# A transformer block on one Trainium2 core: fewer transposes on TensorE, other homes for the key features, and a new order

## The chip, the cores and the metric

The kernel runs on one core of one Trainium2 chip. A core has five engines that run side by side, each through its own queue in order: PE (TensorE, the matrix unit), DVE (VectorE), ACT (ScalarE), POOL (GpSimd) and SP (SyncE, which here only issues DMA transfers). PEld is the part of PE that loads weights. An instruction waits at the head of its queue until the semaphores that it names are reached, and all that stands behind it on that engine waits too. The metric is the device time of one execution, in microseconds; lower is better.

## The reference

The input x has 2048 tokens of 512 numbers. Six vectors of 512 come from silu(c) @ w_mod: sa, ca, ga for the first half and sb, cb, gb for the second.

```python
h = layernorm(x) * (1 + ca) + sa
x = x + ga * A(h)
h = layernorm(x) * (1 + cb) + sb
x = x + gb * B(h)
```

A is attention without a score matrix, with 32 heads of 16:

```python
pq, pk = q @ w_phi, k @ w_phi                      # per head
phi_q = [softmax(pq), softmax(-pq)]                # 32 features per head and token
phi_k = [softmax(pk), softmax(-pk)]
kv, z = phi_k^T v, sum over tokens of phi_k
o = (phi_q kv) / (phi_q z + 1e-6);  A = o @ wo
```

B is (sigmoid(h @ w_gate) * (h @ w_up)) @ w_down, with an inner width of 1376.

## The kernel before

The tokens are 16 tiles of 128, one token per partition. Each piece of work is a small task with a name, a list of engines that it may run on, what it reads and writes, and the buffers that it holds. The text `ORDER` lists all tasks in one sequence; a word such as `xn1_5@P` puts the task on POOL (D is DVE, A is ACT), and a word without a letter takes the first engine of the task's list. The sequence fixes the order of each engine's queue and which buffer a task gets. Nothing is decided at run time.

The stages, with the task names that the text uses (t is a token tile, j one of four blocks of 128 features, g a group of tiles):

- **Loads** `ld_*` on SP, in the order in which SP meets them; SP also issues the DMA transposes, in the same queue.
- **First normalization.** `st1_t` takes mean and variance (DVE, lines 782 and 783). `rs1_g` makes 1/std for a group of tiles, on ACT or POOL (792, 793). `nmr1_g` makes -mean/std, one small DVE instruction per tile (798). `xn1_t` normalizes a tile: on POOL as x times 1/std plus -mean/std (811), on DVE as x minus mean, times 1/std (809), on ACT with scale and bias (807).
- **Transposition and modulation.** The list `LG` says which tiles form a group and `TD` how a group is transposed: 0 by PE (`tphgj`, line 824) into PSUM, 1 by DMA (`xT1_t`, line 816) straight into h1T. Then `hm1_gj` scales and shifts block j of the whole group (831 on ACT, 833 on DVE or POOL). Groups are tiles 0, 1, and then pairs; the pairs 10/11 and 12/13 go by DMA.
- **Weights of q and k** are multiplied by w_phi first (`wTc`, `wqT`, `fold`, `foldc`).
- **Keys.** `Kt` is the key product (850), `et` two exponentials of it on ACT (866), `nt` the softmax sums on DVE (869), `rt` their reciprocals on DVE or ACT (882, 879), `phit` the multiplication of the exponentials by the reciprocals, on POOL (872). `Vt` and `vat` make the values (854, 890). `kvt` adds phi^T v into two PSUM banks (274). From tile 11 on a tile's features are made in two or four parts (`phi11.2` is the part that begins at block 2).
- **kv.** `kvm`, `kvp`, `kvz`, `kvn` mask the finished sum, permute it by a product and store it as `kvbd`.
- **Queries** `Qcb` and their exponentials `qecb` (928, 933) stand in the order wherever PE has room. `modc2` makes the second half's sb and cb, `ga` and `gb` the two gates; `wo*` and `wd*` multiply the gates into the two output weights, on POOL or DVE (908, 917).
- **Attention output.** For tiles 0 to 7 `sm`/`den` make the coefficients and `num`, `u` the weighted sums. For tiles 8 to 15 `num` also holds the denominators; `zti` copies some of its columns to SBUF (367, 369), and `dnt` makes the coefficients from them and the PSUM banks in ten DVE instructions (383 to 391). `ut..` multiplies (433, 435, 450), `ot` adds the two halves on POOL or DVE (468), `oTt` transposes (by DMA from tile 2 on), `outt` is the product with wo (477), `x1_t` the residual.
- **Second normalization and B.** `st2`, `rs2`, `nmr2` (one small DVE instruction per tile, line 504), `xn2`, `xnT`, `mod`, then per chunk of 1, 1, 2, 4, 4 and 4 tiles the products `g` and `u` (568), tanh `tg` (578), `hm` (589), the down-projection `y` (606), `fin` and the store `st`.

A second path for inputs with large scores follows behind a flag; it isn't taken here.

Of the kernel before, what the change touches and what calls it, by code (L numbers as in the profile page):

```python
# [12 lines left out]
ACT = mybir.ActivationFunctionType  # L13
ALU = mybir.AluOpType
AX = mybir.AxisListType

P = 128
# [18 lines left out]
wdz warm0 c1 warm1_0 warm1_1 warm1_2 pmem ld_x0b st1_3 st1_2 bd c2 rs1_2 warm1_3 ld_x0a st1_0 warm1_4 warm1_5 warm1_6 rs1_0 ld_wk ld_x1 st1_1 rs1_1 warm1_7  # L36
tpw3 tpw2 wTc2 tpw0 ld_wm00 ld_wm01 wTc0 tpw1 c3 wTc3@D nmr1_2 warm1_8 warm1_9 warm1_10 warm1_11 warm1_12 warm1_13 xn1_0 nmr1_1 wTc1 fold13 foldc13 xn1_2@P
fold11 fold10 tph03 tph01 fold12 foldc10 foldc11 foldc12 xn1_1@P xn1_3@P st1_5 ld_x2 st1_4 st1_6 st1_7 modc1.0 ld_wv tph02 tph23 tph21 rs1_3@P nmr1_3 modc1.1
modc1c tph20 tph13 warm1_14 tph00 hm1_20 hm1_01@A hm1_21@A hm1_03@A hm1_13 hm1_00 hm1_02 tph22 rs1_4@P nmr1_4 K0 tph10 hm1_22@A hm1_23@A K2 ld_wq st1_11 e0.0
xn1_4@P xn1_5@P xn1_6@P hm1_10@A st1_10 tph11 st1_9 st1_8 e2.0 hm1_11@A tph12 hm1_12@A V2 xn1_7@P tph31 K3 hm1_31 e3.0 tph43 tph30 K1 tph32 rs1_6@P nmr1_6  # L40
n0.0 hm1_43@A rs1_5@P nmr1_5 hm1_32 hm1_30 tph41 V0 tph33 e1.0 tph42 V1 tph40 n2.0 xn1_11@P xn1_10@P ld_x3 wqT3 ld_wo wqT0 r0.0@A hm1_33@A xn1_8@P xn1_9@P
hm1_41 va0 K5 hm1_42@A xT1_11 hm1_40@A va2 va1 tph52 K4 tph53 xT1_10 st1_13 r2.0 n1.0 phi0.0 e4.0 r1.0@A phi2.0 st1_12 tph51 tph50 V4 hm1_50@A hm1_53@A rs1_7
wqT2 phi1.0 n3.0 va4@D hm1_51 hm1_52 wqT1 nmr1_7 xn1_13@P xn1_12@P K6 n4.0 r3.0 r4.0 V3 V5 kv0.0 K7 kv1.0 kv2.0 hm1_62 hm1_61 va5 e5.0 e6.0 n5.0 va3@D e7.0
hm1_63 phi3.0 xT1_13 xT1_12 fold02 V8 r5.0 phi4.0 hm1_60 foldc02 va8 V7 V6 kv3.0 fold00 va7 st1_14 n7.0 r7.0 n6.0 K8 e8.0 phi5.0 hm1_72 K10 kv4.0 fold03 K11
warm1_15 hm1_70@P va6 r6.0@A e11.4 e11.6 hm1_71 kv5.0 phi7.0 hm1_73 n8.0 foldc00@D foldc03@D st1_15 r8.0 e11.0 phi6.0 V11 K9 e11.2 fold01 n11.6 ld_wd2 ld_wd
ld_wu perm e9.0 rs1_8 V10 K13 e13.4 n11.4 foldc01@D n11.2 n9.0 r11.6 nmr1_8 ld_wmga ld_wmm2 r9.0 kv6.0 kv7.0 phi8.0 va10 e10.0 e13.0 va11@D r11.2 V9 va9@D
r11.4 phi9.0 Q00 V12 Q03 xn1_14 xn1_15 qe00 kv8.0 Q10 phi11.2 phi11.4 kv9.0 qe03 n11.0 n10.0 tph81 tph83 phi11.6 r11.0 r10.0@A K12 hm1_81 hm1_83 tph80 tph82
Q13 hm1_82@A phi11.0 phi10.0 hm1_80 n13.0 K15 K14 r13.0 va12@D e12.0 kv10.0 e15.4 phi13.0 n13.4 r13.4@A phi13.4 e15.0 n12.0 r12.0 kv11.4 e14.0 e14.4 n15.4
n14.4 Q02 kv11.0 kv11.2 Q11 V13 ld_wg qe02 qe11 scb kv11.6 r14.4 n15.0 va13@D r15.4 n14.0 phi12.0 r14.0 r15.0 phi14.4 V14 V15 va15 va14 phi15.4 ga kv12.0
kv13.0 modc2.0 kv13.4 kv14.4 kv15.4 phi14.0 qe10 Q01 kvm1 gac kvp2 kvz2 kv14.0 phi15.0 kv15.0 qe01 Q32 kvm0 kvp1 kvp0 qe32 wo1@D wo2 kvz0 kvz1 gb kvn1@A kvn2  # L50
sm0 modc2.1 sm1 modc2c smS1 gbc kvn0 smS0@D qe13 Q12 sm2 num00 num21 num31 num01 den0 wo0 wo3 den1 Q21 qe12 smS2 wo_all wmod_free u00 u01 num11 num30 tpo0 oT0
den2 u31 u30 u11 wd4 Q31 qe31 wd0 wd2 o3 out0 num10 num20 Q23 qe21 x1_0 u10 wd7 wd1 Q30 qe23 st2_0 u21 u20 qe30 rs2_0 Q33 tpo1 sm4 smS4 nmr2_0 oT1@D xn2_0
num60 Q22 num71 qe33 den4 xnT0 out1 oT3 out3 Q20 u71 x1_1 u60 mod00@A mod02@A mod03@A mod01@A x1_3 st2_3 g0.9 g0.0 u0.9 g0.6 u0.0 o2 wd9 tsw tg0.9 tg0.0 oT2
out2 hm0.0 qe20 tg0.6 wd5 g0.5 g0.8 u0.6 wr st2_1 hm0.9 hm0.6 tg0.5 tg0.8 x1_2 u0.5 u0.7 u0.8 hm0.5 hm0.8 wd6 wd10 rs2_1 sm3 g0.1 g0.7 num61 u0.1 qe22 nmr2_1
st2_2 tg0.7 tg0.1 hm0.1 u0.4 wd3 g0.3 u0.3 tg0.3 xn2_1 g0.2 g0.10 g0.4 u61 hm0.3 hm0.7 tg0.4 tg0.2 u0.2 y0.0 rs2_2 hm0.2 nmr2_2 y0.1 xnT1 num70 o6 xn2_3@P
y0.2 y0.3 u0.10 wd8 xn2_2@P mod11 oT6 xnT3 xnT2 hm0.4 num50 y0.4 u70 smS3@D y0.5 y0.6 mod10@A tg0.10 mod13@A mod12@A u1.1 g1.1 y0.7 tg1.1 num51 g1.5 hm0.10
den3 hm1.1 g1.8 g1.9 u1.5 tg1.9 tg1.5 u51 u50 hm1.5 y0.8 y0.9 u1.8 y0.10 fin0 u1.4 g1.4 tg1.4 hm1.4 g1.0 u1.9 u1.0 num41 g1.3 num40 tg1.8 hm1.9 hm1.8 tg1.0
u1.6 u1.3 g1.2 u1.7 mod21@A tg1.3 u40 hm1.0 hm1.3 o7 mod20@A g1.6 tg1.2 tg1.6 hm1.6 u41 u1.10 g1.7 tg1.7 u1.2 o5 out6 mod22@A mod23@P g2.2 oT7 o4@D out7 x1_6
hm1.7 hm1.2 st2_6 x1_7 g2.0 g2.6 u2.0 g2.10 tg2.6 st2_7 tg2.0 st0 oT5 oT4 hm2.0 g1.10 u2.10 u2.6 tg1.10 hm2.6 hm1.10 rs2_4 nmr2_4 g2.1 u2.4 g2.4 tg2.10 hm2.10
num80 z80@D xn2_7@D tg2.4 tg2.1 hm2.4 num81 u2.1 hm2.1 num82 y1.0 out5 z81@D tg2.2 z82 dn8 x1_5 u800 y1.1 y1.2 y1.3 u2.2 hm2.2 xn2_6 xnT7 xnT6 y3.0 out4 g2.8  # L60
g2.5 u2.8 y1.4 tg2.5 y1.5 y1.6 y1.7 y1.8 y1.9 tg2.8 st2_5 x1_4 st2_4 u811 u821 hm2.8 u820 g2.7 y3.1 g2.3 u2.5 rs2_3 u2.3 mod43@A tg2.3 nmr2_3 xn2_5 xnT5 hm2.5
xn2_4@P xnT4 hm2.3 y1.10 num102 z102@D fin1 num92 tg2.7 g2.9 u2.9 num91 num90 y2.0 y2.1 y3.2 tg2.9 z91@D hm2.9 z90 z92 dn9 y3.3 y3.4 u2.7 y2.2 y3.5 y2.3 u900
u921 hm2.7 u911 mod40@P y2.4 y3.6 y2.5 num100 num101 y2.6 mod30@A z101 z100 mod31@P mod42@P mod32@P y2.7 st1 u920 num110 y2.8 y3.7 y2.9 y2.10 o9 dn10 u1021
u1000 fin2 u1011 u1020 o10 o8 y3.8 y3.9 mod33@A mod41@A g3.10 g3.8 u3.10 num130 g3.0 y3.10 tg3.10 z130 tg3.8 hm3.10 fin3 st2 oT9 u3.8 num112 hm3.8 tg3.0 z112
# [12 lines left out]
tg5.5 hm5.5 y9.8 y9.9 y9.10 u5.1 u5.0 g5.0 tg5.1 hm5.1 fin11 fin9 u5.9 u5.10 tg5.0 bndc g5.2 hm5.0 tg5.2 u5.4 g5.9 hm5.4 hm5.2 tg5.9 hm5.9 g5.10 st11 st9
tg5.10 hm5.10 bndd y13.0 y13.1 y13.2 y13.3 y12.0 y12.1 y12.2 y13.4 y13.5 y13.6 y13.7 y13.8 y13.9 y13.10 fin13 st13 y12.3 y12.4 y12.5 y12.6 y12.7 y12.8 y12.9
# [1038 lines left out]
```

## Time and profile before

| | |
|---|---|
| runs | 209.8, 211.09, 211.3 us; median 211.09 |
| the profiled execution | 209.63 us, of which 207.9 are the span from the first instruction to the last |
| PE busy | 200.3 us, 96% of the span, 1516 matmuls |
| DVE busy | 168.2 us, 81%, 459 instructions |
| ACT busy | 107.9 us, 52% |
| POOL busy | 103.4 us, 50% |
| granted PE clock | 1.00 |
| first key product, last matmul | 13.35 and 204.5 us from the start |
| last key feature tile | ends at 56.33 us |

How to read the lines that follow. A line of groups has the source line, the engine, the operation, what it writes and reads by the program's names, the shapes, how often it ran, its busy time, and the mean length of one in ns; behind the bar stands the idle time of the engine in front of it and who ended it. A line of the timeline begins with the start and the length in us. A line of waits has who waited for whom, then us in total, how often, and the longest. Two instructions that follow each other on DVE overlap by about 0.08 us in this trace, so lengths add up to a little more than the time they take.

### The profile page before, as it was taken

Reading aid. Unit: us, or ns where it says so; the run is one execution under the profiler, and the core shown is the slowest. Engines: PE = TensorE matmul, PEld = TensorE weight load, DVE = VectorE, ACT = ScalarE, POOL = GpSimd, SP = SyncE. Lnnn points to the kernel's source line nnn. Section 1 sums busy time; section 2 is a strip of 40 time slices with the busy share of each in tenths; the row PEclk is TensorE's granted clock in tenths of the full one; section 3 lists DMA queues with packets and bytes.
Section 4 is the critical chain, followed back from the end, with each engine's and each line's share of the span. In section 5 each row is a group of like instructions: output and inputs, shape, how many; then the busy total and the mean of one; then the engine's idle time right before and its main releaser. Section 6 shows DMA issues by size and latency. Waiting matters only on the chain.

```text
span 207.9 us, 4302 instructions
## 1 busy us (share of the span) xinstructions
PE 200.3 (96%) x1516; PEld 112.4 (54%) x1539; DVE 168.2 (81%) x459; ACT 107.9 (52%) x259; POOL 103.4 (50%) x137
## 2 busy tenths in 40 slices
PE   7789999999999999999999999999999999999994
PEld 2555465454675588976764544454444444444443
DVE  3999999999599998899988999979797815456642
ACT  2699999999886986524443322521244300142300
POOL 5589999999996989601337202633040612000000
PEclk9999999999999999999999999999999999999999
DMA  6995922999200201522032210342011131001011
GB/s 179 367 349 144 130 32 51 321 390 401 82 3 3 50 2 30 122 33 42 12 76 52 54 25 0 77 101 55 0 29 47 25 79 50 25 2 50 3 60 54
DMA packets 30893, 18.74 MB, mean 90 GB/s; under 512 B 20657, under 2 KB 28818, under 8 KB 30866
## 3 DMA queue, kind: packets, MB, share of 16 engines
q1 hardware_dynamic: 30336, 18.39, 31.6%
q8 instruction: 14, 0.23, 0.5%
q14 instruction: 13, 0.11, 0.2%
q10 hardware_dynamic: 530, 0.02, 0.1%
HBM read 11.58 MB, written 2.10 MB: 66 GB/s over the span
## 4 chain that ended last, share of the span: by engine, by line
PE 74%; ACT 7%; POOL 6%; DMA 4%; DVE 3%; issue 3%; SPq 1%; POOLq 0%; DVEq 0%
PE y_ps L606 18%; PE g_ps L568 17%; PE u_ps L568 17%; PE a_ps L477 6%; POOL phi L872 5%; PE q_ps L928 5%; DMA wmod_sb<-in_w_mod_dram 4%; ACT h1T L831 3%; ACT e L866 2%; DVE ks L869 2%; PE num L360 2%; PE num L444 2%; PE v_ps L854 1%; PE g_ps L570 1%; ACT tg L578 1%
## 5 line engine op out<-in xcount | busy, mean ns | idle before, releaser
L578 ACT ACTIVATE tg<-g_ps 128x512 bf16<-128x512 f32 (+4 forms) x66 | 28.7, 454 | 66.2 <-PE g_ps L568 50.5
L606 PE MATMUL y_ps<-wd_sb,wmod_sb 128*128 128x512 bf16 (+3 forms) x182 | 42.2, 366 | 0.2
L589 DVE SCALAR_TENSOR_TENSOR wmod_sb<-tg,u_ps 128x512 bf16<-128x512 bf16 (+4 forms) x63 | 30.0, 495 | 13.0 <-ACT tg L578 7.0
L872 POOL TENSOR_TENSOR phi<-e,ks 128x1024 bf16<-128x1024 bf16 (+2 forms) x22 | 31.5, 1453 | 0.5
L568 PEld LDWEIGHTS <-wu_sb 128*128 128x128 bf16 (+1 forms) x252 | 21.7, 99 | 15.4
L568 PEld LDWEIGHTS <-wg_sb 128*128 128x128 bf16 (+1 forms) x252 | 21.4, 99 | 15.2 <-issue 0.2
L606 PEld LDWEIGHTS <-wmod_sb 128*128 128x128 bf16 (+1 forms) x187 | 17.9, 98 | 16.5
L568 PE MATMUL g_ps<-wT_sb,wg_sb 128*128 128x512 bf16 (+2 forms) x121 | 23.8, 321 | 0.2
L568 PE MATMUL u_ps<-wT_sb,wu_sb 128*128 128x512 bf16 (+2 forms) x123 | 23.7, 322 | 0.1
L497 POOL TENSOR_SCALAR ve<-mv 128x2 f32<-128x2 f32 (+1 forms) x8 | 1.8, 223 | 41.2 <-DVE mv L487 41.2
L568 PE MATMUL g_ps<-wqk_sb,wg_sb 128*128 128x128 bf16 (+4 forms) x127 | 19.9, 287 | 0.1
L613 DVE TENSOR_TENSOR ot<-y_ps,x 128x512 bf16<-128x512 f32 (+1 forms) x17 | 11.1, 656 | 11.0 <-PE y_ps L606 10.5
L568 PE MATMUL u_ps<-wqk_sb,wu_sb 128*128 128x128 bf16 (+4 forms) x128 | 19.5, 287 | 0.0
L468 POOL TENSOR_TENSOR o<-u 128x512 bf16<-128x512 f32 x12 | 15.2, 1268 | 8.7 <-DVE u L435 4.7
L869 DVE TENSOR_REDUCE ks<-e 128x64 f32<-128x1024 bf16 (+2 forms) x22 | 19.4, 899 | 0.0
L866 ACT ACTIVATE e<-k_ps 128x512 bf16<-128x512 f32 (+2 forms) x44 | 18.1, 502 | 0.3 <-PE k_ps L850 0.2
L933 ACT ACTIVATE eT<-q_ps 128x512 bf16<-128x512 f32 x32 | 17.0, 622 | 1.3 <-PE q_ps L928 1.0
L850 PE MATMUL k_ps<-wqk_f,h1T 128*128 128x512 bf16 x62 | 15.8, 379 | 0.4 <-DVE h1T L833 0.3
L477 PE MATMUL a_ps<-wo_sb,oT 128*128 128x512 bf16 x61 | 15.8, 379 | 0.1
L928 PE MATMUL q_ps<-h1T,wqk_f 128*128 128x512 bf16 x58 | 15.6, 379 | 0.3
L854 PE MATMUL v_ps<-wv_sb,h1T 128*128 128x512 bf16 x62 | 15.6, 379 | 0.2
L782 DVE BATCH_NORM_STATS2 st<-x_sb 128x6 f32<-128x512 bf16 x16 | 10.7, 669 | 2.5 <-DMA x_sb<-in_A_x_dram 2.5
(158 smaller groups left out, 331.3 us busy)
## 6 DMA issues: line engine op xcount, KB each, us to landing
out_dram<-ot SPq DMA_DIRECT2D x15, 128.0 KB, 1.9
x_sb<-in_A_x_dram SPq DMA_DIRECT2D x3, 512.0 KB, 8.5
wmod_sb<-in_w_mod_dram SPq DMA_DIRECT2D x3, 512.0 KB, 7.5
wmod_sb<-in_w_mod_dram SPq DMA_DIRECT2D x1, 1536.0 KB, 14.9
wu_sb<-in_B_w_up_dram SPq DMA_DIRECT2D x1, 1376.0 KB, 9.7
wg_sb<-in_B_w_gate_dram SPq DMA_DIRECT2D x1, 1376.0 KB, 16.4
wd_sb<-in_B_w_down_dram SPq DMA_DIRECT2D x1, 1280.0 KB, 6.6
wqk_sb<-in_A_wqkv_dram SPq DMA_DIRECT2D x2, 512.0 KB, 7.6
```

The lines of the kernel that those rows point to most:

```text
L477: pe.matmul(ap_[:], lhsT=oT[:, j, :], rhs=wo_sb[:, j, :], start=(j == 0), stop=(j == KT - 1))
L568: pe.matmul(ps[:fsz, 0:n], lhsT=w[:, j, ft * P:ft * P + fsz], rhs=h[:, j, 0:n], start=(j == 0), stop=(j == KT - 1))
L578: G.add(f"tg{k}.{ft}", {"ACT": 0.13 + n * 0.00083}, lambda e, tg=tg, g_ps=g_ps, fsz=fsz, n=n: act.activation(tg[:fsz, 0:n], g_ps[:fsz, 0:n ...
L589: dve.scalar_tensor_tensor(hm_all[:fsz, hm[k].slot, ft, 0:n], tg[:fsz, 0:n], 1.0, u_ps[:fsz, 0:n], op0=ALU.add, op1=ALU.mult)
L606: mm = pe.matmul(y[:, 0:c1 - c0], lhsT=hm_all[:fsz, hm[k].slot, ft, tl * P:(tl + 1) * P], rhs=wd_sb[:fsz, ft, c0:c1], start=(ft == 0), sto ...
L850: pe.matmul(kp[:], lhsT=h1T[:, j, t * P:(t + 1) * P], rhs=wqk_f[:, j, D:2 * D], start=(j == 0), stop=(j == KT - 1))
L854: pe.matmul(vp[:], lhsT=h1T[:, j, t * P:(t + 1) * P], rhs=wv_sb[:, j, :], start=(j == 0), stop=(j == KT - 1))
L866: act.activation(ee[:, ha:hb, s, :], kp[:, ha * DH:hb * DH].rearrange("p (h j) -> p h j", j=DH), ACT.Exp, scale=1.0 - 2.0 * s)
L869: dve.tensor_reduce(ks[:, ha:hb].rearrange("p h s -> p (h s)"), ee[:, ha:hb].rearrange("p h s j -> p (h s) j"), axis=AX.X, op=ALU.add)
L872: pool.tensor_tensor(ph[:, ha * 32:hb * 32].rearrange("p (h j) -> p h j", j=DH), ee[:, ha:hb].rearrange("p h s j -> p (h s) j"), ks[:, ha: ...
L928: pe.matmul(qp[:], lhsT=wqk_f[:, j, blk * P:(blk + 1) * P], rhs=h1T[:, j, cq * 512:(cq + 1) * 512], start=(j == 0), stop=(j == KT - 1))
L933: act.activation(eT[cq][:, s * 4 + blk, :], qp[:], ACT.Exp, scale=1.0 - 2.0 * s)
```

## The change

1. **Groups and transposes.** The groups of tiles 8 to 11 and 12 to 15 are now groups of four, and tiles 6 to 15 all go by DMA transposes. PE transposes tiles 0 to 5 alone. `hm1` works on 512 columns in the two groups of four.
2. **Mean.** `xn1` on POOL now subtracts the mean and multiplies by 1/std, as on DVE. `nmr1` stays only for the group that holds tiles 14 and 15 (`XA`), as one instruction for its four tiles; `nmr2` becomes one instruction per pair.
3. **Coefficients.** `z` copies 16 columns per block instead of 8, and `dn` makes the coefficients in six instructions, from the copies alone; the PSUM banks are no longer read by it.
4. **Key features.** `phi` may also run on DVE, as the same multiplication.
5. **Order.** `ORDER` is another sequence. In it `phi6.0`, `phi10.0`, `phi11.6`, `phi13.0`, `phi14.0`, `phi15.0` and `phi15.4` are on DVE, `xn1_11` and `xn1_13` too, and tiles 14 and 15 are normalized on POOL instead of ACT.

SP's queue in the stage of the keys becomes: loads up to the q weights, `xT1_6 xT1_7 ld_x3 wqT0 wqT1 xT1_11 xT1_10 xT1_9 xT1_8 wqT3 wqT2 xT1_13 xT1_12 xT1_14 xT1_15 ld_wd ld_wo ld_wmga ld_wmm2 ld_wd2 ld_wu ld_wg`. Before it was: the same loads and `ld_x3`, then `wqT3 ld_wo wqT0 xT1_11 xT1_10 wqT2 wqT1 xT1_13 xT1_12 ld_wd2 ld_wd ld_wu ld_wmga ld_wmm2 ld_wg`.

```diff
-LG = [[0], [1], [2, 3], [4, 5], [6, 7], [8, 9], [10, 11], [12, 13], [14, 15]]
-TD = [0, 0, 0, 0, 0, 0, 1, 1, 0]
+LG = [[0], [1], [2, 3], [4, 5], [6, 7], [8, 9, 10, 11], [12, 13, 14, 15]]
+TD = [0, 0, 0, 0, 1, 1, 1]
+XA = [14, 15]
...
-                    zS = small("smS", [P, 3, 3, 8])
+                    zS = small("smS", [P, NG, 16])
...
+                    def f_small(e, zS=zS, m=m, den=den, cc=cc):
+                        es = [zS[:, 4 * s:4 * s + 4, 8:16] for s in range(2)]
                         for s in range(2):
-                            dve.tensor_tensor(mq[s], part(s, 0), zS[:, 1 - s], op=ALU.mult)
-                        for s in range(2):
-                            dve.tensor_tensor(mq[2][:, s, :], part(2, 0)[:, s, :], zS[:, 2, 1 - s, :], op=ALU.mult)
-                        dve.tensor_reduce(den[:, 0], m[:, 0].rearrange("p (s h) -> p h s", h=32), axis=AX.X, op=ALU.add)
+                            dve.tensor_tensor(m[:, 0, 32 * s:32 * s + 32].rearrange("p (b n) -> p b n", n=8), zS[:, 4 * s:4 * s + 4, 0:8], es[1 - s], op=ALU.mult)
+                        dve.tensor_tensor(den[:, 0], m[:, 0, 0:32], m[:, 0, 32:64], op=ALU.add)
                         dve.reciprocal(den[:, 0], den[:, 0])
...
+                            dve.tensor_tensor(cc[:, 0, s].rearrange("p (b n) -> p b n", n=8), es[1 - s], den[:, 0].rearrange("p (b n) -> p b n", n=8), op=ALU.mult)
...
-                    for t in tiles:
-                        dve.tensor_scalar(nmr[:, 1, t:t + 1], mv2[:, t, 0:1], rs2[:, t:t + 1], -1.0, op0=ALU.mult, op1=ALU.mult)
+                    sl = slice(tiles[0], tiles[-1] + 1)
+                    dve.scalar_tensor_tensor(nmr[:, 1, sl], mv2[:, sl, 0], -1.0, rs2[:, sl], op0=ALU.mult, op1=ALU.mult)
...
-        if g:
+        if any(t in XA for t in ts):
...
-                elif e == "DVE":
-                    dve.tensor_scalar(xn[:], x_sb[:, t, :], mv1[:, t, 0:1], rs1[:, t:t + 1], op0=ALU.subtract, op1=ALU.mult)
                 else:
-                    pool.tensor_scalar(xn[:], x_sb[:, t, :], rs1[:, t:t + 1], nmr[:, 0, t:t + 1], op0=ALU.mult, op1=ALU.add)
+                    engine(e).tensor_scalar(xn[:], x_sb[:, t, :], mv1[:, t, 0:1], rs1[:, t:t + 1], op0=ALU.subtract, op1=ALU.mult)
...
-                pool.tensor_tensor(ph[:, ha * 32:hb * 32].rearrange("p (h j) -> p h j", j=DH), ee[:, ha:hb].rearrange("p h s j -> p (h s) j"),
+                engine(e).tensor_tensor(ph[:, ha * 32:hb * 32].rearrange("p (h j) -> p h j", j=DH), ee[:, ha:hb].rearrange("p h s j -> p (h s) j"),
                                    ks[:, ha:hb].rearrange("p h s -> p (h s)").unsqueeze(2).to_broadcast([P, 2 * (hb - ha), DH]), op=ALU.mult)
```

The rest of the diff is the text of `ORDER` and the durations by which it was written.

More of the change, by code (lines that the diff above doesn't have):

```diff
@@ L37 @@
[L37 to L52, printed above, removed]
@@ L834 @@
             if TD[g]:
-                w = {"DVE": 0.17 + 0.035 * n, "ACT": 0.25 + 0.11 * n, "POOL": 0.12 + 0.165 * n}
-                G.add(f"hm1_{g}{j}", {e: w[e] for e in ("ACT", "POOL")}, f_m, r=[("h1raw", t) for t in ts] + ["mod1"],
+                w = {"DVE": 0.171 + 0.035 * n, "ACT": 0.25 + 0.11 * n, "POOL": 0.12 + 0.165 * n}
+                G.add(f"hm1_{g}{j}", w, f_m, r=[("h1raw", t) for t in ts] + ["mod1"],
                       w=[("h1", g, j)], port=("POOL", "DVE"))
```

105 lines of the change are left out of this document (55 added, 50 removed).

## The prediction

> **What bounds the kernel now.** I read the page's totals first: TensorE (PE) is busy for 96% of the span. That average hides the stages, so next I asked for the busy time in five stretches, cut at the first key product (13.3), the first masked copy of the finished key/value sum that the chain goes through (56.7), the first down-projection (81), and the last matmul (204.7).
>
> ```profile
> span 207.9 us, 4302 instructions
> ...
> PE 200.3 (96%) x1516; PEld 112.4 (54%) x1539; DVE 168.2 (81%) x459; ACT 107.9 (52%) x259; POOL 103.4 (50%) x137
> ```
>
> ```profile
> 13.30:56.70 43.40, 42.87 (x354) 23.12 (x362) 40.38 (x86) 41.64 (x105) 42.59 (x43) 1.00 0.68 204
> 56.70:81.00 24.30, 24.07 (x308) 17.07 (x311) 22.95 (x63) 20.09 (x51) 21.15 (x23) 1.00 0.07 13
> 81.00:141.00 60.00, 59.63 (x446) 36.87 (x451) 55.38 (x196) 23.09 (x61) 22.47 (x30) 1.00 0.25 54
> 141.00:204.70 63.70, 63.34 (x313) 29.71 (x316) 39.80 (x86) 15.18 (x26) 8.84 (x15) 1.00 0.14 37
> ```
>
> The columns are the length, then PE, weight loads, DVE, ACT, POOL, the granted clock, the DMA share and GB/s. The reader is to see two things. PE never rests from 13.3 to 204.7: a matmul taken off it pays in full, and any wait put on it is lost in full. And in the first stretch, where the keys are made, DVE (40.4 of 43.4), ACT (41.6) and POOL (42.6) are all full too. There a wait on any of them soon reaches PE. The waits by line show that POOL's key features are already the ones that come last:
>
> ```profile
> PEld L274 <- POOL phi L872: 2.0, 6, 0.5
> ...
> DVE kvm L295 <- POOL phi L872: 1.4, 1, 1.4
> ```
>
> The last feature tile ends at 56.33 on POOL and the last key/value product starts at 56.38.
>
> **What one operation costs.** From the groups kept apart by shape, and from the timeline of POOL and DVE around 57 and 141:
>
> ```profile
> L872 POOL TENSOR_TENSOR phi<-e,ks 128x1024 bf16<-128x1024 bf16 x12 | 23.1, 1929 | 0.4
> L869 DVE TENSOR_REDUCE ks<-e 128x64 f32<-128x1024 bf16 x12 | 14.3, 1195 | 0.0
> ```
>
> ```profile
> 56.28 1.17 POOL L908 TENSOR_TENSOR wo_sb<-wo_sb,ga_sb 128x512 bf16<-128x512 bf16 x1
> 57.08 0.92 DVE L908 TENSOR_TENSOR wo_sb<-wo_sb,ga_sb 128x512 bf16<-128x512 bf16 x1
> 57.39 1.62 POOL L908 TENSOR_TENSOR wo_sb<-wo_sb,ga_sb 128x512 bf16<-128x512 bf16 x1
> 58.98 1.16 POOL L908 TENSOR_TENSOR wo_sb<-wo_sb,ga_sb 128x512 bf16<-128x512 bf16 x1
> ```
>
> ```profile
> 140.97 0.81 DVE L468 TENSOR_TENSOR o<-u 128x512 bf16<-128x512 f32 x1
> 141.23 0.98 POOL L545 TENSOR_SCALAR wqk_sb<-wqk_sb,modc 128x256 bf16<-128x256 bf16 x1
> ```
>
> Here is what I think decides the case. One DVE multiply of two SBUF operands (57.08) ends 0.55 us after POOL's first multiply ends (57.45), though 512 elements alone take 0.69 (shortest of L468); POOL's next one, begun at 57.39, takes 1.62 instead of 1.16 and ends 1.02 after DVE's. At 141 POOL's 0.56 us operation takes 0.98 while DVE adds two SBUF operands. So a DVE instruction with two SBUF operands and a POOL instruction exclude each other. The sums L869 with one operand don't: they hold 1.16 to 1.22 beside features that stay at 1.93. A multiply phi on DVE has two SBUF operands (e and ks), like wo.
>
> The Trainium skill ("SBUF — State Buffer", Who interferes with whom) says the same of two SBUF inputs against a GpSimd instruction that reads SBUF, and lets one that only writes go free; the trace agrees on the first, and shows nothing on the second. By its rule the one-column instruction for -mean/std of tiles 12 to 15, now also of two SBUF inputs, would queue behind a whole feature tile, up to 1.93 us; no row here has so small a one beside POOL, and the sum below goes without it.
>
> **Part by part.**
>
> *Transposes.* Tiles 6 to 9, 14 and 15 leave PE: 6x4 matmuls of 128 columns, 0.056 us each in the queue (the chain has "tp_h x4" at 0.22): -1.34 us on the bound. Six DMA transposes of 1.21 come to SP, 7.3 us. Queued behind them are the load of the last x tiles (behind the second one; wanted by statistics some 5 us later) and those of wd, wo and the last of w_mod, wu and wg. These were issued at 34.6 to 38.7 and now wait for the transpose of tile 15, about 38. At the 390 GB/s of that stage the 6.6 MB end near 56; the first gate matmul was at 73. Cost 0; without that cover, each us late is a us.
>
> *Modulation of the transposed tiles.* Groups of four make it 12 instead of 20 instructions from tile 6 on. ACT: 13 (0.57 and 0.62) become 2 of 0.62 and 4 of about 0.86 (the nearest, L807, 128x512): -3 us. DVE: -8 of 0.40 net of one. POOL: +2 of 0.56 and 4 of 0.78 (L811) in place of one of 0.56: +3.7.
>
> *Subtracting the mean on POOL.* Same instruction, shape and two pointers: 0.777 before and after, 0. What goes is its wait for DVE (2.3 us once) and 14 of 15 small DVE instructions of 0.198, 2.8 us. Next late is the reciprocal standard deviation, on POOL itself.
>
> *Key features on DVE.* POOL sheds 2x1.93 + 4x1.06 + 0.62 = 8.7 us. DVE gets 2x1.22 + 4x0.69 + 0.42 = 5.6 (0.69 for 512 elements, of which 0.53 is data since wo ended 0.55 after its lock; so 1.07 and 0.27 for the others). Bounds for the lock: nothing, if the partners never meet; or per feature tile one whole POOL instruction in flight: 2x1.93 + 0.62 + 1.06 + 3x0.8 = 7.9 us of DVE.
>
> *The key stage as a sum.* DVE in total is about even (5.6 in, plus two normalizations of 0.41 and ga's copy of 0.65; 3.2 of modulations, 2.8 of small ones, and some copies out). PE: the new order has 2.1 us less in front of the last key/value product (1.34 of transposes, the product modc2.0 of 0.40, kvp2 of 0.13, a warm-up matmul of 0.22), so unhindered PE is there at 56.38 - 2.1 = 54.3. The locked pair: the first feature tile started at 21.07, since its sum ended at 18.65 on DVE, its reciprocal only at 20.36 on ACT, behind other work, and POOL had two normalizations left. In the new order one modulation and two small ones (0.7) are gone from in front of the sum and the reciprocal (0.53) follows on DVE at once; POOL has these two normalizations behind or none left: 18.5, with the hand-over 18.7. From there to the last feature tile POOL has 31.9 us in the new order (10x1.95, 3x0.57, 2x1.03, 4 normalizations 3.0, 6 modulations 4.2, the 1.3 for perm and the issue between them), and DVE's feature tiles block it for their data, 2x1.07 + 4x0.53 + 0.27 = 4.5. That is 18.7 + 36.4 = 55.1 with POOL never idle. It does idle: features 4, 7, 11 and 12 each wait for a reciprocal that stands in DVE's queue behind a locked-out feature tile (7 behind none, 11 behind tile 10, 12 behind 13.0), some 2.4 us together. So the last one at 57.5, and PE stands still for 3.2. Against 56.38 that is +1.1, and behind it PE has 0.53 more left than before (modc2.0 and kvp2): **+1.6 us**.
>
> *Six-instruction coefficients, fused mean factors.* Per tile 1.51 becomes about 1.25: five of 0.18 to 0.2 and a reciprocal of 0.35; 8x0.26 = 2.1 us off DVE, in stretches where PE is the bound: gain 0. But their operands are now all in SBUF, so each may be held by POOL (37% busy from 81 to 141) for up to 1.27. From both sides: 0, and 1.27x8 = 10 minus DVE's idle 4.6 and the 2.1 saved, 3.5. Nearer to nothing, as matmuls of four other tiles lie between: +0.6.
>
> *Start and end.* The first key product still waits for the second half of w_mod, sixth load as before (landed 11.3), and for as much DVE work; the last matmul's tail of 3.4 is untouched: 0.
>
> **Sum.** 1.6 + 0.6 = +2.2: span 210.1, execution 209.63 + 2.2 = 211.8. The median of the runs shown, 211.09, lies 1.46 above the profiled one (209.8 to 211.3); by it 213.3. I give 212.5, between the two.
>
> **Rivals.**
>
> 1. *The lock costs nothing* (ends on the other side). Partners meet rarely, or PE has other work while DVE waits. For: POOL sheds 5.0 net, DVE is even. Against: POOL is 98% busy there. PE keeps its 1.34: 208.3 to 209.8 by the two bases. It decides if the last feature tile ends by 54.5. That the change misses its aim is part of this: the fused instruction of tiles 12 to 15 feeds nothing, as their normalization no longer runs on ACT.
>
> 2. *The group of four is late.* Keys 12 to 15 all need tiles 12 to 15. Their last normalization ends near 36.5; two transposes (2.4) and a landing (2.4 to 4.3, h1T) give 41 to 43, then three POOL modulations of 0.78, so 43.5 to 45.5, where PE wants key 13 at 42.6. With the lock's wait behind it, +3 to +5.5: 213 to 216.5.
>
> 3. *PE gets ahead at the start*: would need the sixth load sooner; nothing in the queue speaks for it. -2.2 or more: below 207.4.
>
> **How the numbers follow.** Forecast 0.50 (211 to 214), rival 1 0.27, rival 2 0.18, rival 3 0.05. One per cent, 2.1 us, is about what a measurement tells from no change. The forecast's upper half and rival 2 are beyond it: 0.52 slower; rival 1 and the lower half 0.43; faster 0.05. The range leaves out the lower part of rival 1 with rival 3, and the top of rival 2: 208.4 to 216.
>
> **What would show it.** Right: phi on DVE at 1.5 us or more instead of 1.22 where POOL runs, POOL features above 1.93, PE waiting 2 to 5 us for phi before 58. Wrong: both groups at their own lengths and the last key/value product before 55.

## The result and the profile after

The changed kernel takes 229.66 us (median of four runs, 229.25 to 229.76) against 210.44 for the kernel before (four runs, 209.73 to 211.3): ratio 1.091, interval 1.085 to 1.096, that is 19.2 us slower. The forecast was 212.5 in a range of 208.4 to 216. The record below has one run in the slower state of the chip (226.97 us, of the kernel with multiply-add and all features on POOL), which no median or ratio here includes.

The page's totals of the changed kernel, and the clock row of its 40 slices:

```profile
span 228.0 us, 4202 instructions
...
PE 204.5 (90%) x1490; PEld 112.1 (49%) x1515; DVE 172.1 (75%) x405; ACT 108.5 (48%) x256; POOL 114.6 (50%) x130
...
PEclk9999589999999999999999999999999999999999
```

PE went from 96% of the span to 90%: the span is 20 us longer, with 24 matmuls fewer in the program (the records lack a few in both). One slice shows the clock at half. The busy time by stretch, cut at the first key product (14.62), the end of the first long stall (24.80), the end of the half clock (31.0), the last key/value product (72.70), the first down-projection (97.70) and the last matmul; the columns are as in the prediction:

```profile
14.62:24.80 10.18, 3.78 (x22) 1.56 (x21) 5.28 (x13) 5.40 (x13) 9.99 (x14) 0.94 0.35 92
24.80:31.00 6.20, 6.20 (x23) 2.81 (x24) 4.36 (x8) 4.19 (x10) 6.01 (x5) 0.55 0.25 48
31.00:72.70 41.70, 34.26 (x269) 17.39 (x273) 34.47 (x54) 32.52 (x81) 37.61 (x30) 1.00 0.56 175
72.70:97.70 25.00, 24.24 (x330) 17.49 (x332) 23.36 (x62) 18.56 (x45) 21.58 (x20) 1.00 0.21 51
97.70:224.40 126.70, 124.58 (x759) 66.81 (x770) 94.87 (x246) 41.70 (x95) 28.36 (x41) 1.00 0.19 42
```

Before, PE, DVE, ACT and POOL were all full in the key stage. Now POOL alone is full through the first 16 us: it works 16.0 of 16.4 us, while PE, DVE and ACT are busy for 3.8, 5.3 and 5.4 of the first 10.2. The loss lies in the first three rows. What POOL does there, from the groups kept apart by shape; the first line is the normalization of before, the second that of the changed kernel, the third answers to L872 of before:

```profile
L811 POOL TENSOR_SCALAR xn<-x_sb,rs,nmr 128x512 bf16<-128x512 bf16 x13 | 9.9, 777 | 2.3 <-DVE nmr L798 2.3
...
L799 POOL TENSOR_SCALAR xn<-x_sb,mv,rs 128x512 bf16<-128x512 bf16 x13 | 27.1, 2089 | 0.2
L860 POOL TENSOR_TENSOR phi<-e,ks 128x1024 bf16<-128x1024 bf16 x10 | 19.2, 1932 | 1.2 <-DVE ks L870 1.2
```

One normalization takes 2.089 us instead of 0.777: 13 of them put 17.1 us on POOL, three of them just ahead of the key stage and ten in it. The waits by line show who paid:

```profile
PE tp_h L812 <- POOL xn L799: 7.4, 2, 6.3
...
PEld L274 <- POOL phi L860: 3.5, 4, 2.5
```

The last feature tile ends at 72.05 instead of 56.33. By the start of the first key product, of the last key/value product and of the last matmul (from the timelines), the kernel falls into stretches that depend little on when the key stage begins, which differs by up to 2.8 us among the profiled executions below. (In three kernels that have before's key stage, from 13.35, 13.93 and 14.52 on, it took 43.14, 43.17 and 43.13; in three that have that of the add-multiply kernel below, from 13.15, 13.28 and 15.85 on, 46.06, 45.94 and 45.44.)

| kernel | first key product | to the last key/value product | from there to the last matmul |
|---|---|---|---|
| before | 13.35 | 43.14 | 148.04 |
| changed | 14.62 | 58.10 | 151.46 |

So +15.0 in the key stage, +3.4 behind it, +1.3 at the start, which lies within those 2.8, and +0.5 at the end: the 20.1 between the spans. The experiments below take these apart; their tables use the same two stretches, called keys and rest.

### The profile page after: what moved, and what is told of

It is laid out like the page before. It is cut to its first block, busy times and chain, and to the rows that moved or that the text cites. A ratio compares the mean times of both kernels' runs of the same rounds, so it can differ in the third digit from the quotient of the medians.

```text
span 228.0 us, 4202 instructions
## 1 busy us (share of the span) xinstructions
PE 204.5 (90%) x1490; PEld 112.1 (49%) x1515; DVE 172.1 (75%) x405; ACT 108.5 (48%) x256; POOL 114.6 (50%) x130
## 4 chain that ended last, share of the span: by engine, by line
PE 49%; DVE 21%; POOL 17%; issue 6%; DMA 3%; ACT 2%; SPq 1%; POOLq 0%; DVEq 0%; ACTq 0%
PE u_ps L558 14%; PE g_ps L558 13%; PE y_ps L596 13%; POOL xn L799 9%; DVE ks L857 4%; POOL phi L860 4%; PE a_ps L467 3%; DVE u L440 2%; DVE phi L860 1%; PE num L360 1%; POOL rs L783 1%; DMA x_sb<-in_A_x_dram 1%; PE q_ps L916 1%; DVE ks L870 1%; DVE wmod_sb L579 1%
## 5 line engine op out<-in xcount | busy, mean ns | idle before, releaser
L568 ACT ACTIVATE tg<-g_ps 128x512 bf16<-128x512 f32 (+5 forms) x66 | 29.1, 455 | 60.8 <-PE g_ps L558 45.9
L596 PE MATMUL y_ps<-wd_sb,wmod_sb 128*128 128x512 bf16 (+3 forms) x182 | 44.1, 366 | 0.2
L558 PEld LDWEIGHTS <-wu_sb 128*128 128x128 bf16 (+1 forms) x252 | 21.7, 99 | 14.9 <-issue 0.2
L799 POOL TENSOR_SCALAR xn<-x_sb,mv,rs 128x512 bf16<-128x512 bf16 x13 | 27.1, 2089 | 0.2
L860 POOL TENSOR_TENSOR phi<-e,ks 128x1024 bf16<-128x1024 bf16 (+2 forms) x15 | 23.8, 1599 | 3.3 <-DVE ks L870 2.5
L558 PE MATMUL u_ps<-wqk_sb,wu_sb 128*128 128x256 bf16 (+4 forms) x128 | 19.8, 287 | 0.1
L921 ACT ACTIVATE eT<-q_ps 128x512 bf16<-128x512 f32 x32 | 17.4, 607 | 5.1 <-PE q_ps L916 3.6
L458 POOL TENSOR_TENSOR o<-u 128x512 bf16<-128x512 f32 x11 | 14.0, 1274 | 9.2 <-DVE u L425 6.3
L838 PE MATMUL k_ps<-wqk_f,h1T 128*128 128x512 bf16 x63 | 16.8, 396 | 1.4 <-POOL h1T L821 1.4
L842 PE MATMUL v_ps<-wv_sb,h1T 128*128 128x512 bf16 x60 | 16.9, 408 | 0.2
```

The lines of the kernel that those rows point to most:

```text
L558: pe.matmul(ps[:fsz, 0:n], lhsT=w[:, j, ft * P:ft * P + fsz], rhs=h[:, j, 0:n], start=(j == 0), stop=(j == KT - 1))
L568: G.add(f"tg{k}.{ft}", {"ACT": 0.13 + n * 0.00083}, lambda e, tg=tg, g_ps=g_ps, fsz=fsz, n=n: act.activation(tg[:fsz, 0:n], g_ps[:fsz, 0:n ...
L596: mm = pe.matmul(y[:, 0:c1 - c0], lhsT=hm_all[:fsz, hm[k].slot, ft, tl * P:(tl + 1) * P], rhs=wd_sb[:fsz, ft, c0:c1], start=(ft == 0), sto ...
L799: engine(e).tensor_scalar(xn[:], x_sb[:, t, :], mv1[:, t, 0:1], rs1[:, t:t + 1], op0=ALU.subtract, op1=ALU.mult)
L842: pe.matmul(vp[:], lhsT=h1T[:, j, t * P:(t + 1) * P], rhs=wv_sb[:, j, :], start=(j == 0), stop=(j == KT - 1))
L860: engine(e).tensor_tensor(ph[:, ha * 32:hb * 32].rearrange("p (h j) -> p h j", j=DH), ee[:, ha:hb].rearrange("p h s j -> p (h s) j"), ks[: ...
```

## The experiments

**One instruction form in the kernel before.** All else is the kernel before; only POOL's normalization has the changed form.

```diff
-    pool.tensor_scalar(xn[:], x_sb[:, t, :], rs1[:, t:t + 1], nmr[:, 0, t:t + 1], op0=ALU.mult, op1=ALU.add)
+    pool.tensor_scalar(xn[:], x_sb[:, t, :], mv1[:, t, 0:1], rs1[:, t:t + 1], op0=ALU.subtract, op1=ALU.mult)
```

> The kernel before with one edit: the thirteen normalizations on GpSimd subtract the mean and multiply, instead of multiplying and adding; order, groups and all small instructions stay. Theory S (the form is slow on GpSimd: in the changed kernel the thirteen took 2.09 us each instead of 0.78, 17.1 us more in all): normalizations near 2.07 us here too, and as GpSimd is full from 13 to 57, the time rises by 10 to 18 us, to 220 to 228. Rival L (the normalizations only look long in the changed kernel, because VectorE holds the port that GpSimd needs): 0.77 us each as before, and no change of the time.

Measured 224.36, ratio 1.065 (1.060 to 1.071): +13.9 us from one line. The group of this kernel:

```profile
L811 POOL TENSOR_SCALAR xn<-x_sb,mv,rs 128x512 bf16<-128x512 bf16 x13 | 26.8, 2076 | 0.1
```

The keys took 56.87 (43.14 before), the rest 148.05 (148.04). So the form is slow by itself, in the old order too, where no feature runs on DVE; what DVE does beside it is not the reason.

**Which part of the form.** Seven forms, twice each, on POOL near the end of the kernel before, with nothing else changed in the computation; measured once, 210.36 us.

```diff
+    pool.tensor_scalar(pscr[:], x, m_, r_, op0=ALU.subtract, op1=ALU.mult)    # L942
+    pool.tensor_scalar(pscr[:], x, r_, n_, op0=ALU.mult, op1=ALU.add)         # L943
+    pool.tensor_scalar(pscr[:], x, m_, None, op0=ALU.subtract)                # L944
+    pool.tensor_scalar(pscr[:], x, r_, None, op0=ALU.mult)                    # L945
+    pool.tensor_scalar(pscr[:], x, n_, r_, op0=ALU.add, op1=ALU.mult)         # L946
+    pool.tensor_scalar(pscr[:], x, r_, n_, op0=ALU.mult, op1=ALU.subtract)    # L947
+    pool.tensor_scalar(pscr[:], x, 0.5, 2.0, op0=ALU.subtract, op1=ALU.mult)  # L948
```

> The kernel before, with fourteen added instructions on GpSimd near the end, where it is idle and no transfer waits for it: seven forms of one 128x512 bf16 operation, twice each, into a scratch tile that nobody reads. They tell what in the form is slow. Theory S1 (the subtraction): forms with subtract near 2.07, multiply-add and add-multiply near 0.77. Theory S2 (a pointer for the first operand together with another for the second in this order): add-multiply with two pointers slow as well. Theory S3 (nothing about the form): all near 0.77. The time of the kernel: no change beyond 1 per cent.

```profile
L942 POOL TENSOR_SCALAR pscr<-x_sb,mv,rs 128x512 bf16<-128x512 bf16 x2 | 4.2, 2080 | 0.1
L947 POOL TENSOR_SCALAR pscr<-x_sb,rs,nmr 128x512 bf16<-128x512 bf16 x2 | 4.1, 2072 | 0.2
L948 POOL TENSOR_SCALAR pscr<-x_sb 128x512 bf16<-128x512 bf16 x2 | 3.9, 1932 | 0.2
L944 POOL TENSOR_SCALAR pscr<-x_sb,mv 128x512 bf16<-128x512 bf16 x2 | 3.1, 1562 | 0.2
L945 POOL TENSOR_SCALAR pscr<-x_sb,rs 128x512 bf16<-128x512 bf16 x2 | 3.1, 1562 | 0.2
L943 POOL TENSOR_SCALAR pscr<-x_sb,rs,nmr 128x512 bf16<-128x512 bf16 x2 | 1.5, 768 | 0.2
L946 POOL TENSOR_SCALAR pscr<-x_sb,nmr,rs 128x512 bf16<-128x512 bf16 x2 | 1.5, 762 | 0.2
```

The reader is to see that neither the order of the two operations nor the pointers decide: multiply-add and add-multiply take 0.77, the same with a subtraction 2.07 to 2.08, and 1.93 with constants in place of the pointers. One operation alone, even a single multiplication, takes 1.56, twice the fast pair. None of the three theories had that. So it isn't that the subtraction is slow in itself; among these seven only the two pairs of multiply and add are fast. Why was not tested.

**The changed kernel with a fast form.** First with before's form, multiply-add, and -mean/std for it from DVE.

```diff
-    engine(e).tensor_scalar(xn[:], x_sb[:, t, :], mv1[:, t, 0:1], rs1[:, t:t + 1], op0=ALU.subtract, op1=ALU.mult)
+    pool.tensor_scalar(xn[:], x_sb[:, t, :], rs1[:, t:t + 1], nmr[:, 0, t:t + 1], op0=ALU.mult, op1=ALU.add)
```

> The changed kernel with one edit undone: GpSimd multiplies by 1/std and adds -mean/std again, with one small VectorE instruction per tile for that product, as in the kernel before. Groups of four, key features on VectorE, coefficients and order stay. Theory S: the normalizations fall to 0.77 us and nearly all of the 19 us goes; what stays is what my prediction had for the rest, 211 to 214. Rival L (the lock between two-operand VectorE instructions and GpSimd is most of the loss): still above 222. Rival G (the groups of four and the order): also above 222.

220.09, ratio 1.048 (1.039 to 1.056): short of the 211 to 214 of the first theory and of the 222 of the others. POOL's normalizations are at 785 ns again, but POOL waits 4.5 us for the small DVE instructions that this form needs, and for which the new order was not made:

```profile
L801 POOL TENSOR_SCALAR xn<-x_sb,rs,nmr 128x512 bf16<-128x512 bf16 x13 | 10.1, 785 | 4.5 <-DVE nmr L788 4.5
```

The other fast form needs no DVE: x plus -mean, times 1/std, with -mean by one small POOL instruction per group. That is the changed kernel's own computation and order with the price that I had assumed, and with six small POOL instructions more (0.25 to 0.33 us each by their groups' means).

```diff
-    dve.scalar_tensor_tensor(nmr[:, 0, sl], mv1[:, sl, 0], -1.0, rs1[:, sl], op0=ALU.mult, op1=ALU.mult)
+    pool.tensor_scalar(nmr[:, 0, sl], mv1[:, sl, 0], -1.0, None, op0=ALU.mult)
...
-    engine(e).tensor_scalar(xn[:], x_sb[:, t, :], mv1[:, t, 0:1], rs1[:, t:t + 1], op0=ALU.subtract, op1=ALU.mult)
+    pool.tensor_scalar(xn[:], x_sb[:, t, :], nmr[:, 0, t:t + 1], rs1[:, t:t + 1], op0=ALU.add, op1=ALU.mult)
```

> The changed kernel with its thirteen GpSimd normalizations written as (x + (-mean)) times 1/std, a form that took 0.762 us in the probe, and -mean made by one small GpSimd instruction per group from the statistics alone. So GpSimd again waits for nobody's -mean/std, as the change intended, but at the price that my prediction had for it. If the price of the form is the only wrong term: 211 to 214, and the 4.5 us that GpSimd waited for VectorE's small instructions in the multiply-and-add run are gone, with the PE wait of 3.3 at 20.4. If the rest of the change (lock, groups of four, order) is worth more than my +2.3: 216 to 220.

216.52, ratio 1.028 (1.024 to 1.032). The form, net of the six small instructions, thus costs the changed kernel 13.1 us of its 19.2; 6.1 are left. Keys 46.06 (+2.9 on before), rest 151.77 (+3.7). The long stall near 20 is gone. POOL's normalizations, and PE's two longest waits between 13 and 60 us:

```profile
L800 POOL TENSOR_SCALAR xn<-x_sb,nmr,rs 128x512 bf16<-128x512 bf16 x13 | 10.9, 849 | 0.2
```

```profile
PE kvacc L273 <- POOL phi L861: 2.4, 1, 2.4
PE kvacc L273 <- DVE phi L861: 0.6, 1, 0.6
```

The mean is 849 ns and not 762 because one of the thirteen took 1.85 us, beside a feature on DVE (see the lock below).

Some differences among the next kernels are the clock's. In several profiled executions, though not in this one, the granted clock of PE is at half for 3.4 us, and then PE's work there takes twice as long; the text says where that lies in a stretch that it compares.

**Groups of four.** The same kernel with tiles 8 to 15 in four pairs, all by DMA, so eight more modulations, and two more instructions of each kind that makes 1/std and -mean.

```diff
-LG = [[0], [1], [2, 3], [4, 5], [6, 7], [8, 9, 10, 11], [12, 13, 14, 15]]
+LG = [[0], [1], [2, 3], [4, 5], [6, 7], [8, 9], [10, 11], [12, 13], [14, 15]]
```

> The last kernel with tiles 8 to 15 in four pairs instead of two groups of four, all still by DMA transposes; each word of the order that named a group now names its two pairs one after the other. Theory G (keys 12 to 15 wait for a whole group): 1 to 3 us faster than the last kernel, keys 12 and 13 earlier. Otherwise: 0.5 to 2 us slower, from eight modulations more (0.56 to 0.62 each on GpSimd and ACT in place of half of 0.77 to 0.81).

219.63, ratio 1.042 (1.037 to 1.048), 3.1 us slower than with groups of four, 2.4 of it in the keys (48.44). About 1.4 of the 3.1 may be the clock: the profiled execution has it at half from 60.5 to 63.8, around the end of the keys, and the one of the four runs whose clock was full (0.999) took 218.25, 1.7 more than 216.52. The groups of four help.

**Key features on DVE, priced from both orders.** In the kernel before, the same seven features go to DVE and nothing else changes (`phi6.0` becomes `phi6.0@D`, and so on).

> The kernel before with one part alone: the same seven key features on VectorE, in their places of the old order. GpSimd sheds 8.7 us, VectorE takes 5.6 and waits for the feature tile that GpSimd is at. Lock theory: phi on VectorE up to 3.1 us instead of 1.21, the last key feature near 56 or later, 0 to +3 us. If the lock's waits are hidden: GpSimd's relief shows, last key feature before 54, time the same within 0.5 per cent, since PE is the bound and has no less to do.

214.35, ratio 1.019 (1.015 to 1.023): +4.0, beyond the 0 to +3 of the lock theory, keys 46.76 (+3.6). The lock, the waiting of POOL and of DVE's two-operand instructions for each other, is not what costs that. The longest of the seven features takes 1.50 instead of 1.16, another 1.08 instead of 0.67, so they lose some 0.7 us to it in all. But DVE is now busy for 45.6 of the 46.8 us of the keys, and POOL for only 37.0 (40.3 and 42.3 of 43.1 before): the features went to the engine that thereby became the fullest. In the changed kernel, the opposite edit, all features back on POOL, once with each fast form.

> The last kernel with all seven key features on GpSimd again, in the same places of the order. If the lock costs more than the relief brings: faster than the last kernel. By my sums GpSimd then has 31.9 + 8.7 = 40.6 us from the first feature tile at 18.7, so the last would end near 59.5 instead of 57.5: 2 us slower than the last kernel, 213 to 216. No feature tile on VectorE, so no multiplication there above its own length.

> Changed kernel with the fast form, all key features on GpSimd again, same sequence otherwise. GpSimd gets 8.7 us more, the vector engine sheds 5.6 and all its lock waits. Theory that the new order needs the moved features (as beside the mult-add form, where they were worth 4.4 us): 219 to 221.5. Rival, that the lock eats what the move brings: 215 to 217.

With multiply-add 224.15 (the median of the other three runs; ratio 1.063, 1.055 to 1.072) against 220.09, so the features on DVE gain 4.1 there, where 213 to 216 had been expected; with add-multiply 219.45 (1.044, 1.040 to 1.049) against 216.52, 2.9 of gain, 3.2 in the keys, as expected this time. In this last pair too the clock has a part: it is at half from 49.8 to 53.1 in the kernel without features on DVE, and the one of its six runs with a full clock (0.999) took 218.63, 2.1 more than 216.52. The same edit loses 4 us in one order and gains 2 to 4 in the other. In the new order POOL has more to do (modulations, all of tiles 14 and 15): with all features on it, it is busy for 47.0 of the 49.3 us of the keys and DVE for 35.5, with seven on DVE for 41.3 and DVE for 42.2 of 46.1. There the edit levels two engines that it sets apart in the old order.

**What is late at the end of the keys.** In the kernel with add-multiply, `perm` stands between the last features on POOL and takes 2.43 us there. It was moved behind `phi14.4`.

```diff
-... r14.4@A perm phi15.4@D ld_wmga ... phi14.0@D phi14.4 Q13
+... r14.4@A phi15.4@D ld_wmga ... phi14.0@D phi14.4 perm Q13
```

> Changed kernel with the fast form, and the building of the permutation on GpSimd (perm, 2.43 us there, 1.48 alone) moved from in front of the last key features to behind phi14.4. Theory that the locked-out GpSimd work beside the last vector features is what makes the last feature late: phi14.4 ends 1.5 to 2.5 us earlier (58.5 becomes 56 to 57), TensorE's stall of 2.5 us at 58.6 shrinks to under 1.2, time 214.9 to 215.8. Rival, that the last feature is late because of its chain on the vector engine (sums and reciprocals): phi14.4 ends within 0.7 of 58.5 and the time is 216 to 217.

217.43, ratio 1.033 (1.029 to 1.037), no gain; keys 45.94 against 46.06. The rest is 153.15 against 151.77, with the clock at half from 58.9 to 62.2; the three of the six runs with a full clock took 216.49 to 217.29. POOL and DVE around the last feature of that kernel:

```profile
52.62 1.93 POOL L861 TENSOR_TENSOR phi<-e,ks 128x1024 bf16<-128x1024 bf16 x1 [1.15 <-DVE ks L871]
56.83 1.57 POOL L861 TENSOR_TENSOR phi<-e,ks 128x512 bf16<-128x512 bf16 x1 [2.29 <-ACT eT L922]
```

```profile
52.40 2.40 DVE L858 TENSOR_REDUCE ks<-e 128x32 f32<-128x512 bf16 x4
54.71 0.55 DVE L871 RECIPROCAL ks<-ks 128x32 f32<-128x32 f32 x2
55.37 2.12 DVE L861 TENSOR_TENSOR phi<-e,ks 128x512 bf16<-128x512 bf16 x3
```

POOL now stands idle for 2.3 us, and `phi14.4` starts at 56.83 all the same. The page names ACT as releaser, but the instruction also waits for DVE, whose second of the three features ended at 56.66. That it is DVE is inferred: `phi14.4` starts 0.17 us behind that feature here and in the kernel before this edit (56.96 behind 56.79), while its distance from ACT's instruction differs. So the last feature is late by the chain on DVE: four sums, two reciprocals, two features. The rival holds, though the time is 0.4 above its 217. The lock's part at the end is the 0.5 us by which `phi14.4` (1.57 instead of 1.06) is stretched beside DVE's third feature; a little earlier, in DVE's chain itself, a feature of 512 columns at 50.76 takes 1.26 instead of 0.69.

**The small instructions.** In the kernel before, change 3 and the `nmr2` part of change 2 alone:

> The kernel before with two parts of the change alone: six-instruction coefficients from copies in SBUF, and one instruction per pair for the second normalization's -mean/std. My prediction has +0.6 us for the waits of two-operand instructions for GpSimd, bounds 0 and 3.5. If the lock decides: instructions of the coefficients that take up to 1.3 us where GpSimd works, and 0 to 1.5 us in all. If it doesn't: within 0.5 per cent of before.

211.89 against 210.26 in the same session (ratio 1.006, 1.003 to 1.009): +1.3 by the ratio, keys 43.13 (0), rest 149.37 (+1.33). In the changed kernel with add-multiply, the old ten-instruction coefficients:

> Changed kernel with the fast form on GpSimd, and the old ten-instruction coefficients that read PSUM. Theory that the six-instruction form costs here what it cost in the old order (1.3 us, through the lock with GpSimd's second-half work): 215.0 to 215.6 beside 216.5, and the 1.28 us stall of TensorE near 117.6 gone or under 0.5. Rival, that the stalls of the second half come from the new order alone: 216.3 to 217, the stall stays.

217.56, ratio 1.034 (1.030 to 1.039): no gain, and above both expectations. This run, that with `perm` moved and that with add-multiply and all features on POOL were made in a later session than the kernel that they are held against. The profiled execution of this one has the clock at half from 9.0 to 12.3, and its first key product stands at 15.85 instead of 13.15; the one of its six runs with a full clock took 216.37, within the 216.01 to 216.72 of the other kernel. In the stretches, the keys are 45.44 against 46.06 and the rest is 151.44 against 151.77. The stall of 1.28 us at 117.6 did shrink to 0.24, but four others of 0.2 to 0.3 came in its place. So what the coefficients cost in the old order is not what makes the rest long in the new one.

**Add-multiply in the kernel before.** The second edit in the best form that I found, in the old order.

> Kernel before, old order, with the normalization on GpSimd in the other fast form: x plus (-mean), times 1/std; -mean by one small GpSimd instruction per group (about 0.25 us, seven of them), so the small vector instructions for -mean/std of tiles 1 to 13 are gone and GpSimd no longer waits for them (2.3 us once). What the change could have had from its second edit alone. If the form is the whole matter: normalizations at 0.76 to 0.80 us, and the wait gone weighs against 1.8 us of new small instructions on a full GpSimd: 209.5 to 211.5 beside 210.4. If the subtraction itself (or the dependence on the mean) were slow: 220 or more.

211.90, ratio 1.008 (1.005 to 1.010), a little beyond the expected 209.5 to 211.5: no gain, though the 2.3 us wait of POOL for DVE is gone. The keys took 44.63 (+1.5, with the clock at half from 14.9 to 18.2), the rest 148.59 (+0.5). None of the parts that were tried alone makes the kernel before faster, and no mixture of them promised to, so none was tried. The groups of four and the DMA transposes were not tried in the old order, and the new order not without the other parts.

## Why the prediction was wrong

**The step that failed** is *Subtracting the mean on POOL*: "Same instruction, shape and two pointers: 0.777 before and after, 0". It measured 2.089. Instruction, shape and pointers were the same, and the pair of operations was not. I took the row of another form as the price, and as it looked like the same instruction I gave no second end, although the trace of before holds no subtraction of this size on POOL. With one, for instance POOL's slowest row of 512 columns in that trace (`o`, L468, 1.27 us), the upper end would have been 6.4 us on POOL and still short of the truth, 17.1; but the step would have stood in the text as an unknown. Of the +19.2 it is 13.1, shown twice: by undoing it in the changed kernel and by doing it alone in the kernel before (+13.9).

The Trainium skill ("GPSIMD Engine Reference", 3.1 Elementwise — side-by-side cycle accounting) gives 769 ns as measured for 512 elements, as the best case of a tight loop. The trace agrees for the two pairs of multiply and add (768 and 762) and not for the rest: one operation at 1562, two with a subtraction at up to 2080. The measurement decides.

**The remaining sum** can be held against the kernel with add-multiply, which is +6.1 where the sum said +2.2. Stalls of PE are counted from start to start of its matmuls, beyond their usual distance; the idle times in the views are about 0.16 shorter.

- *Transposes* (-1.34): the changed kernel's trace has 11 of these matmuls behind the first key product, before's has 35. The 24 are gone as counted, and the queue of SP held nothing up: no engine waits for a load from memory behind the first key product.
- *The key stage as a sum* (+1.1 at its end, by a wait of 3.2): the wait for the last feature is there, 2.5 us at 58.58, and that feature ended at 58.53 where I had 57.5. The sum missed what came earlier: PE stood 0.6 at 17.4, 0.5 at 24.7, 0.4 at 41.6, 0.4 at 44.0 and 0.8 at 47.7, so keys of 46.1 against the 44.2 of my sum. The first feature tile started at 20.9, not 18.7: its reciprocal ended at 18.70, as I had it, but POOL still had 1/std of a group of four (1.3 us) and two normalizations (1.5) to do, which I had put behind the feature, and one of the six small instructions (0.4). I let one chain end last and gave all other waits nothing, in a stage where four engines are full.
- *The rest* (+0.5 of moved work and +0.6): measured +3.7. The moved work is 0.5 by the records, as I had it (16 matmuls of `modc2.0` 0.025 apart, four of `kvp2` 0.03 apart). Stalls of 0.66 at 83.8, 1.28 at 117.6 and 0.4 at 151.8 make most of the others. The first is the wait for tile 0's second normalization; the second has no releaser on the page.
- *Six-instruction coefficients, fused mean factors* (+0.6, bounds 0 and 3.5): +1.3 in the old order. Inside the bounds, undersized. The 2.1 us that I took off DVE are not there either: the ten instructions kept it busy for 1.41 us a tile before, not 1.51, and the six for 1.39, as three of theirs took 0.46 to 1.21 instead of 0.19.

**The lock** was read rightly for POOL's multiplications of two operands, and too widely for POOL's other work. The timeline of the changed kernel, DVE and then POOL:

```profile
41.94 1.21 DVE L857 TENSOR_REDUCE ks<-e 128x64 f32<-128x1024 bf16 x1
...
43.99 1.88 DVE L788 SCALAR_TENSOR_TENSOR nmr<-mv,rs 128x4 f32<-128x4 f32 x1
...
48.59 1.21 DVE L860 TENSOR_TENSOR phi<-e,ks 128x1024 bf16<-128x1024 bf16 x1
...
58.37 2.83 DVE L860 TENSOR_TENSOR phi<-e,ks 128x1024 bf16<-128x1024 bf16 x1
```

```profile
40.10 5.76 POOL L860 TENSOR_TENSOR phi<-e,ks 128x1024 bf16<-128x1024 bf16 x3
45.85 6.19 POOL L799 TENSOR_SCALAR xn<-x_sb,mv,rs 128x512 bf16<-128x512 bf16 x3
...
58.18 1.93 POOL L860 TENSOR_TENSOR phi<-e,ks 128x1024 bf16<-128x1024 bf16 x1
```

The instruction of four columns for -mean/std begins at 43.99 and ends at 45.87, 0.01 behind the feature tile that POOL had in flight. By the rule of the Trainium skill ("SBUF — State Buffer", Who interferes with whom) it was to wait for the whole feature tile; the trace agrees, 1.88 of at most 1.93. I had called it one-column and left it out of the sum, and it feeds nothing, as the prediction said. The feature tile on DVE at 58.37 takes 2.83 where the same shape at 48.59, beside no feature, takes 1.21: it runs after POOL's, not beside it. The sum at 41.94, with one operand, keeps its 1.21 beside a POOL feature, as read from before. So the bound of nearly one whole POOL instruction for a locked feature tile is real.

But the feature at 48.59 lies wholly beside POOL's subtract-multiply normalizations, three of 2.07 from 45.85 on, and neither side is longer than alone. With add-multiply it is otherwise (DVE, then POOL, of that kernel):

```profile
35.93 1.21 DVE L861 TENSOR_TENSOR phi<-e,ks 128x1024 bf16<-128x1024 bf16 x1
```

```profile
35.19 3.34 POOL L800 TENSOR_SCALAR xn<-x_sb,nmr,rs 128x512 bf16<-128x512 bf16 x3
```

Three normalizations take 3.34 us there, beside a feature of its own length, and 2.27 at 8.13, beside none. So not every POOL instruction excludes DVE's two operands, as the prediction and that rule have it: the slow form did not in the one pair that shows it, and the fast form did. Why is open.

Of the signs that I named, DVE features over 1.5 and a wait of 2 to 5 us for the last feature are there (2.5, though 14 us later than I had it); POOL's whole tiles stayed at 1.93, and only its parts were stretched (1.57 instead of 1.06, 0.80 instead of 0.62).

**The rivals.** *The lock costs nothing* fell by its own sign: with add-multiply the last feature tile ends at 58.53, not by 54.5, and DVE's features are some 2.2 us longer there than by themselves (2.83 for 1.21, 1.26 for 0.69). The +4.0 of the old order says nothing on it, as the lock took 0.7 there. Its reason, that POOL sheds more than DVE takes, was right in the new order (2 to 4 gained), where other things cost more. *The group of four is late* fell: with add-multiply the key product of tile 13 waits 0.4 us, and pairs are 3.1 us slower. *PE ahead at the start* fell.

What stays open: the split of the rest's 3.7 us by cause beyond the 0.5 of moved work, and how much of the small waits of PE in the keys each part of the new order makes.

## What to carry to other kernels

The price of an instruction belongs to its exact form, the pair of operations included: where the trace has no row of that form, it is an unknown to be bounded or measured by itself, however alike a neighbouring row looks, and one that runs 13 times on a full engine deserves that first. A move of work between two engines is worth what the fuller one sheds in this order, so it can lose 4 us in one sequence and gain 2 to 4 in another. In a stage where several engines are full, a sum along the one chain that ends last left out 2.7 us of small waits before it, which must be added.

## What the runs showed of the hardware

- GpSimd's multiply-add and add-multiply by two pointers take 0.76 to 0.77 us for 128x512; a single multiplication or subtraction takes 1.56, and a pair with a subtraction 1.93 (constants) to 2.08. Doing more can be twice as fast.
- A stall of PE costs more than its length. Around the end of the 6.35 us at 24.78 the granted clock was 0.50, from 23.5 to 30.3, and products of 512 columns came 0.427 apart instead of 0.216, at least eleven times: some 2.3 us more. The timeline of PE in the changed kernel, four products in 1.03 ahead of the stall and in 1.91 behind it:

```profile
17.41 1.03 PE L838 MATMUL k_ps<-wqk_f,h1T 128*128 128x512 bf16 x4
24.78 0.82 PE L812 MATMUL tp_h<-ident,xn 128*128 128x128 bf16 x6 [6.35 <-POOL xn L799]
25.39 1.91 PE L838 MATMUL k_ps<-wqk_f,h1T 128*128 128x512 bf16 x4
```

- The same short stall is followed by the half clock in one kernel and not in another: PE's wait of 2.3 to 2.4 us for the last feature was, for 3.4 us, in the kernels with pairs (from 60.5) and with `perm` moved (from 58.9), and was not in the changed kernel (72.1) and with add-multiply (58.6), whose clock stayed at 1.00. So two kernels can differ by about 1.4 us in one execution by the clock alone.
- An instruction of four columns with two SBUF operands can cost DVE as much as a whole feature tile of POOL, 1.88 us; the fused one-column -mean/std of the second normalization took 1.13 at 95.1, where those of two columns take 0.15 by themselves.
- DVE's two-operand feature (1.21 us) ran beside POOL's subtract-multiply without a loss on either side, and stretched POOL's add-multiply from 0.76 to 1.85.
